# Scores and second GEMM on half-height row tiles of TensorE, with the steps, the sums and the last transposed x put in a new order

## The chip, the cores and the metric

One core of one Trainium2 chip. The metric is the device time of the whole kernel in microseconds, the median of several executions. Besides the times I use one profiled execution of each kernel. From its trace I take one number above all, which I call the **pitch** of a block: from the start of its first score matmul to the start of the next block's. It lets a change in one block be read apart from the other blocks. (Block 7 has no next block; its attention half takes as long as those of blocks 3 to 6.)

## The reference, cut to what matters

Decayed causal attention over 8 batches of 8 heads (576 tokens, head size 64), then a feed-forward layer of 512 to 2048 to 512 with exact GELU over all 4608 tokens.

```python
scores = scale * np.matmul(q, k.transpose(0, 1, 3, 2))      # q, k: (8, 8, 576, 64)
decay = cum[:, :, :, None] - cum[:, :, None, :]             # cum = cumsum(log f)
scores = np.where(causal, -1000000000.0, scores + decay)
attn = softmax(scores)                                      # over the keys
x = np.matmul(attn, v)  ->  (4608, 512)
h = x @ w_in                                                # 512 -> 2048
out = (0.5 * h * (1.0 + erf(h * inv_sqrt2))) @ w_out        # 2048 -> 512
```

## The kernel before

The program walks over blocks: block b is batch b. Each block has an attention half and a half in which TensorE runs the first GEMM of that block and ScalarE the GELU. The second GEMM of block b-1 is cut into 64 single matmuls of 512 columns, and these *steps* are dealt out among the score tiles of block b, so that TensorE has work while ScalarE takes the exponentials. Two heads lie in one 128-partition tile, one in each half. A score has a contraction of 64, so the other half of the query tile is zeroed and each head gets a full 128-row matmul:

```python
qA = [consts.tile([P, S], BF16, name=f"qA{i}") for i in range(HP)]   # lower half zero
qB = [consts.tile([P, S], BF16, name=f"qB{i}") for i in range(HP)]   # upper half zero
kT = [consts.tile([P, S], BF16, name=f"kT{i}") for i in range(HP)]

def scores(b, i, t):                       # head pair i, tile t of 4
    st = s_psum.tile([P, 2, 512], FP32, tag="s", name=f"s{t}")       # two buffers
    c = 0
    for n, q0, w in STILES[t]:             # 256+192, 320+128, 448, 320 columns
        for h, qt in enumerate((qA[i], qB[i])):
            nc.tensor.matmul(st[:, h, c : c + w], kT[i][:, K0[n] : K0[n] + P],
                             qt[:, q0 : q0 + w], ...)
        ...                                # block 0 and pair 0 of block 1: mask matmuls, 128 rows
        c += w
    nc.scalar.activation(et[:, :, 0:c], st[:, :, 0:c], Act.Exp, scale=scale)
    ...                                    # else: the mask by GpSimd on et
```

```python
def gemm2(c, quarters=False):              # a generator: one step at each yield
    ...
        nc.tensor.matmul(pss[ts], g_of[c][kt][:, ts * P : (ts + 1) * P],
                         w_out_sb[:, kt, :], start=(kt == 0), stop=(kt == n_ff - 1))
        if kt == n_ff - 1:
            nc.vector.tensor_copy(ot, pss[ts]);  nc.sync.dma_start(out[...], ot)
        yield

FILL = [[4, 6, 2, 2], [2, 2, 2, 2], [2, 2, 2, 2], [2, 2, 1, 1], [8, 0, 20]]
# steps after tile t of pair i; the attention product of pair i-1 goes in three pieces
# after tiles 1, 2 and 3 of pair i; the last x goes through a transposing DMA under 20 steps
```

Block 1 has its own table of steps, as its weights still arrive. The last piece, the tails of 64 tokens, follows after block 7 and isn't touched.

The softmax here doesn't subtract the row's maximum and nothing guards it: scores larger than these inputs give would overflow.

## Time and profile before

| | before |
|---|---|
| time, median of 3 | 357.31 us (356.77 to 357.79) |
| TensorE busy | 97% of the span |
| pitch of blocks 1, 2, 3 to 7 | 40.81, 38.14, 37.42 us |
| attention half and first GEMM of a block from 3 on | 23.53 and 13.89 us |
| VectorE and ScalarE busy in such an attention half | 9.37 and 16.23 us |

How to read it: matmuls are pipelined, so the lengths in a timeline overlap (a 512-column matmul lasts 379 ns and the next starts after 216). I read prices from starts. A share of 97% says only that TensorE always has something in flight. The prediction shows the lines.

### The profile page before, as it was taken

To read this page: it belongs to the slowest core of one execution; us is meant where nothing else is said; L and a number is where in the kernel's file an instruction comes from. 1 tells how busy PE (TensorE), PEld (TensorE's weight loads), DVE (VectorE), ACT (ScalarE), POOL (GpSimd) and SP (SyncE) were. 2 spreads that over 40 slices of the span, in tenths; PEclk is the share of its full clock that TensorE was granted. 3 is DMA by queue.
4 is the path that set the end of the run, shared out by engine and by line. 5 is a ranking of instruction groups with operands and counts; after the bars stand their busy time and mean duration, and the time that the engine had idled before them with its cause. 6 is when DMAs were issued, how large, how long until landed. Compare 5 with 4: busy or idle time off the path is not lost.

```text
span 356.2 us, 7069 instructions
## 1 busy us (share of the span) xinstructions
PE 346.8 (97%) x2756; PEld 190.7 (54%) x2756; DVE 182.1 (51%) x482; ACT 217.4 (61%) x298; POOL 124.5 (35%) x243
## 2 busy tenths in 40 slices
PE   8998989999999999999999999999999999999995
PEld 3784556544664466445654565446544664444443
DVE  6771984595467625781559145924584361011011
ACT  5697586368854797279826882688457854603600
POOL 7390275406546044804470256215520530000000
PEclk9999999999999999999999999999999999999999
DMA  7999999885997894489639973979310132011013
GB/s 116 169 188 191 190 155 202 183 192 90 205 158 161 146 185 122 95 142 189 144 98 134 188 139 82 174 141 173 76 66 2 45 61 81 2 59 59 2 30 88
DMA packets 103936, 43.85 MB, mean 123 GB/s; under 512 B 82720, under 2 KB 99360, under 8 KB 103904
## 3 DMA queue, kind: packets, MB, share of 16 engines
q1 hardware_dynamic: 86608, 29.26, 40.4%
q0 software_dynamic: 16896, 13.63, 25.6%
q10 hardware_dynamic: 400, 0.52, 0.4%
q8 instruction: 21, 0.34, 0.4%
q14 instruction: 11, 0.09, 0.1%
HBM read 36.85 MB, written 9.44 MB: 130 GB/s over the span
## 4 chain that ended last, share of the span: by engine, by line
PE 94%; ACT 2%; DMA 1%; issue 1%; DVE 1%; POOL 0%; ACTq 0%; DVEq 0%; POOLq 0%
PE ps L404 35%; PE ps L442 35%; PE s L308 13%; PE o L344 8%; ACT e L323 2%; PE ps_f L198 1%; DMA k<-in_k_dram 1%; PE s L317 1%; PE ps_w L187 1%; PE ps_x L380 0%; PE s_t L233 0%; PE ps_t L233 0%; DVE x L360 0%; ACT xt L368 0%; ACT g L416 0%
## 5 line engine op out<-in xcount | busy, mean ns | idle before, releaser
L416 ACT ACTIVATE g<-ps 128x512 bf16<-128x512 f32 x144 | 86.0, 597 | 97.9 <-PE ps L404 97.8
L442 PE MATMUL ps<-w_out_sb,g 128*128 128x512 bf16 (+2 forms) x592 | 143.8, 373 | 0.0
L323 ACT ACTIVATE e<-s 128x896 bf16<-128x896 f32 (+1 forms) x128 | 105.1, 863 | 19.8 <-PE s L308 11.3
L404 PE MATMUL ps<-xT,w_in_sb 128*128 128x512 bf16 x512 | 112.9, 379 | 0.7 <-ACT xT L383 0.6
L325 POOL TENSOR_SCALAR_AFFINE_SELECT e<-e 128x256 bf16<-128x256 bf16 x135 | 53.7, 408 | 118.6 <-ACT e L323 117.7
L404 PEld LDWEIGHTS <-w_in_sb 128*128 128x128 bf16 x576 | 56.0, 97 | 69.2 <-issue 3.9
L451 DVE COPY ot<-ps 128x512 f32<-128x512 f32 (+2 forms) x37 | 25.1, 677 | 105.3 <-PE ps L442 105.0
L442 PEld LDWEIGHTS <-g 128*128 128x128 bf16 x592 | 52.2, 98 | 41.8
L292 POOL TENSOR_TENSOR vw<-v_sb,wT 128x640 bf16<-128x640 f32 x32 | 41.0, 1282 | 45.7 <-PE ps_t L233 15.9
L308 PEld LDWEIGHTS <-kT 128*128 128x128 bf16 x384 | 36.7, 98 | 33.3 <-issue 6.2
L308 PE MATMUL s<-qA,kT 128*128 128x256 bf16 (+2 forms) x192 | 51.9, 282 | 2.1 <-ACT e L323 2.0
L308 PE MATMUL s<-qB,kT 128*128 128x256 bf16 (+2 forms) x192 | 48.6, 282 | 0.0
L344 PE MATMUL o<-vw,e 128*128 128x65 bf16 x960 | 43.5, 194 | 0.5 <-ACT e L323 0.4
L344 PEld LDWEIGHTS <-e 128*128 128x128 bf16 x960 | 39.5, 98 | 7.5 <-ACT e L323 0.5
L359 DVE RECIPROCAL r<-o 128x5 f32<-128x5 f32 x64 | 12.5, 195 | 41.5 <-PE o L344 41.0
L276 DVE COPY kT<-tk 64x288 bf16<-64x288 bf16 x96 | 32.3, 336 | 1.4
L360 DVE TENSOR_TENSOR x<-o,r 128x256 bf16<-128x256 f32 x64 | 27.2, 425 | 2.4 <-DVE r L359 0.2
L276 DVE COPY qB<-tq 64x288 bf16<-64x288 bf16 x48 | 18.8, 391 | 0.6
L370 DVE TENSOR_SCALAR xt<-o,r 64x64 bf16<-64x64 f32 x60 | 17.5, 291 | 1.4
L276 DVE COPY qA<-tq 64x288 bf16<-64x288 bf16 x48 | 17.1, 355 | 1.1
L404 PE MATMUL ps<-tails,w_in_sb 128*128 128x512 bf16 x64 | 14.4, 377 | 0.0
L416 ACT ACT_TABLE_LOAD x8 | 10.3, 1283 | 0.1
(63 smaller groups left out, 124.4 us busy)
## 6 DMA issues: line engine op xcount, KB each, us to landing
out_dram<-ot SPq DMA_DIRECT2D x32, 256.0 KB, 2.2
v_sb<-in_v_dram SPq DMA_DIRECT2D x20, 256.0 KB, 4.7
v_sb<-in_v_dram SPq DMA_DIRECT2D x29, 128.0 KB, 5.4
q<-in_q_dram POOLq DMA_DIRECT2D x6, 576.0 KB, 6.6
k<-in_k_dram POOLq DMA_DIRECT2D x6, 576.0 KB, 9.0
w_in_sb<-in_moe_w_in_dram POOLq DMA_DIRECT2D x4, 512.0 KB, 7.6
w_out_sb<-in_moe_w_out_dram POOLq DMA_DIRECT2D x4, 512.0 KB, 9.6
q<-in_q_dram POOLq DMA_DIRECT2D x4, 144.0 KB, 4.1
```

The lines of the kernel that those rows point to most:

```text
L276: nc.vector.tensor_copy(rows[:, odd], src[odd * D : (odd + 1) * D, 2 * i + h].rearrange("d j p -> d p j"),)
L292: nc.gpsimd.tensor_tensor(vw_of[b][:, hs, :, 0:D], v_sb[:, hs, :, :], w.unsqueeze(3).to_broadcast([P, 2, NBLK, D]), Alu.mult,)
L308: nc.tensor.matmul(st[:, h, c : c + w], kT[i][:, K0[n] : K0[n] + P], qt[:, q0 : q0 + w], start=True, stop=not on_pe or c not in SDIAG[t],)
L323: nc.scalar.activation(et[:, :, 0:c], st[:, :, 0:c], Act.Exp, scale=scale)
L325: nc.gpsimd.affine_select(out=et[:, :, c0 : c0 + P], in_=et[:, :, c0 : c0 + P], compare_op=Alu.is_ge, fill=0.0, base=0, pattern=[[0, 2], [ ...
L344: nc.tensor.matmul(o[:, m, :], e_of[b, i, t][:, h, c : c + P], vw_of[b][:, 2 * i + h, n, :], start=(n == 0), stop=(n == m),)
L360: nc.vector.tensor_tensor(x_of[b, i][:, :, h, :], o[:, 0:4, 0:D], r[:, 0:4].unsqueeze(2).to_broadcast([P, NBLK - 1, D]), Alu.mult,)
L370: nc.vector.tensor_scalar(*tail, r[D:P, 4:5], None, Alu.mult)
L404: nc.tensor.matmul(ps, w_in_sb[:, kt, ffb * P : (ffb + 1) * P], src[:, kt, :], start=(kt == 0), stop=(kt == n_dm - 1),)
L416: nc.scalar.activation(g_of[c][ffb], ps, Act.Gelu)
L442: nc.tensor.matmul(pss[ts][:, c0:c1], g_of[c][kt][:, ts * P : (ts + 1) * P], w_out_sb[:, kt, c0:c1], start=(kt == 0), stop=(kt == n_ff - 1),)
L451: nc.vector.tensor_copy(ot[:, c0:c1], pss[ts][:, c0:c1])
```

## The change

The intent: a head's score needs only 64 of the array's 128 rows, so two heads can use the upper and the lower half at the same time. But a change between whole-height and half-height matmuls costs time (0.095 us in the trace before; I call it a drain), so the steps dealt out between score tiles are made half-height as well: each contraction of 128 is split into two of 64 ("r"), summed in two banks (parts of the memory that TensorE writes to), and VectorE adds the two for each token tile (128 tokens of the output). A few steps ("n") stay whole, where they stand beside the attention product, which is whole.

```diff
-    qA = [consts.tile([P, S], BF16, name=f"qA{i}") for i in range(HP)]
-    qB = [consts.tile([P, S], BF16, name=f"qB{i}") for i in range(HP)]
+    qT = [consts.tile([P, S], BF16, name=f"qT{i}") for i in range(HP)]
...                                        (zeroing memsets go; copies of q write qT)
-            for h, qt in enumerate((qA[i], qB[i])):
+            for h in range(2):
+                d = slice(h * D, (h + 1) * D)
                 nc.tensor.matmul(
                     st[:, h, c : c + w],
-                    kT[i][:, K0[n] : K0[n] + P],
-                    qt[:, q0 : q0 + w],
+                    kT[i][d, K0[n] : K0[n] + P],
+                    qT[i][d, q0 : q0 + w],
...
+    STEPS = [
+        16 * "r",
+        5 * "r" + 2 * "n" + 8 * "r" + "n",
+        9 * "r" + 2 * "n" + 5 * "r",
+        8 * "r" + 8 * "n",
+    ]
+    def gemm2_rows(c):
+        for ts, steps in enumerate(STEPS):
+            ...                            (two banks: of o for ts 0, of m for 1 and 2, of s for 3)
+            for kt, step in enumerate(steps):
+                last = kt == steps.rindex("r")
+                for r in range(2 if step == "r" else 1):
+                    rows = slice(r * D, (r + 1) * D) if step == "r" else slice(0, P)
+                    nc.tensor.matmul(banks[r], g_of[c][kt][rows, ...], w_out_sb[rows, kt, :], ...)
+                if kt == n_ff - 1 if ts == n_sub - 1 else last:
+                    nc.vector.tensor_copy(ot, banks[1])
+                if kt == n_ff - 1:
+                    nc.vector.tensor_tensor(ot, ot, banks[0], Alu.add)
+                    nc.sync.dma_start(out[...], ot)
+                yield
...
-    FILL = [[4, 6, 2, 2], [2, 2, 2, 2], [2, 2, 2, 2], [2, 2, 1, 1], [8, 0, 20]]
+    FILL = [[6, 5, 4, 3], [0, 3, 3, 2], [0, 3, 3, 3], [0, 3, 3, 2], [8]]
+    FILL_AV = [2, 1, 2, 2]
...
+        def av(i):                         (whole product of a pair, after tile 1 of the next)
+            for h in range(2):
+                attend(b, i, h, (0, 1, 2, 3, 4))
+                if h == 0:
+                    take(fill, FILL_AV[i])
+                normalize(b, i, h)
...
-            x_dma(b, i)                    (last x, blocks 3 to 7; 20 steps behind it)
+        av(HP - 1)
+        take(fill, 5)
+        to_xT(b, HP - 1, nc.vector.tensor_copy, o_psum, "o")     (four transposes, one copy)
+        take(fill, 999)                                          (one step)
```

Blocks 0 and 1 get the half-height scores too, but block 1 keeps its old order and, as its steps, the whole-height second GEMM of block 0. The second GEMM of block 7, behind all attention, stays whole-height too.

More of the change, by code (lines that the diff above doesn't have):

```diff
@@ L142 @@
     make_identity(nc, ident_fp)
-    qA = [consts.tile([P, S], BF16, name=f"qA{i}") for i in range(HP)]
-    qB = [consts.tile([P, S], BF16, name=f"qB{i}") for i in range(HP)]
+    qT = [consts.tile([P, S], BF16, name=f"qT{i}") for i in range(HP)]
     kT = [consts.tile([P, S], BF16, name=f"kT{i}") for i in range(HP)]
-    def zero_halves(pairs):
-        for i in pairs:
-            nc.vector.memset(qA[i][D:P, :], 0.0)
-            nc.vector.memset(qB[i][0:D, :], 0.0)
     w_in_sb = consts.tile([P, n_dm, d_ff], BF16)
@@ L174 @@
     nc.vector.memset(ones, 1.0)
-    zero_halves(range(2))
     nc.vector.memset(wT[0:D, 4, :], 0.0)
@@ L202, in transposes_first @@
                 )
-        def evac(eng, dst, r0, r1):
-            op = eng.copy if eng is nc.scalar else eng.tensor_copy
-            op(
-                dst[r0:r1, :].rearrange("d (p j) -> d p j", j=JT),
-                ps[r0:r1].rearrange("d j p -> d p j"),
-            )
-        if which:
-            evac(nc.vector, kT[i], 0, P)
-        else:
-            evac(nc.vector if i else nc.scalar, qA[i], 0, D)
-            evac(nc.vector, qB[i], D, P)
+        op = nc.scalar.copy if i == 0 and not which else nc.vector.tensor_copy
+        op(
+            (qT, kT)[which][i].rearrange("d (p j) -> d p j", j=JT),
+            ps.rearrange("d j p -> d p j"),
+        )
     def transposes_pe(b, i, pool):
@@ L239, in transposes_pe @@
             for h in range(2):
-                dst = (qA[i], qB[i])[h] if which == 0 else kT[i]
+                dst = (qT, kT)[which][i]
                 rows = dst[h * D : (h + 1) * D, :].rearrange(
@@ L270, in untangle @@
             for h in range(2):
-                dst = (qA[i], qB[i])[h] if which == 0 else kT[i]
+                dst = (qT, kT)[which][i]
                 rows = dst[h * D : (h + 1) * D, :].rearrange(
@@ L461, in gemm2 @@
             yield
+    STEPS = [
[6 more added lines that the diff above has]
+        for ts, steps in enumerate(STEPS):
+            if ts < n_sub - 1:
+                pool, tag = (m_psum, "m") if ts else (o_psum, "o")
+                banks = [
+                    pool.tile([P, d_model], FP32, tag=tag, name="ps2")
+                    for _ in range(2)
+                ]
+            else:
+                both = s_psum.tile([P, 2, d_model], FP32, tag="s", name="ps2")
+                banks = [both[:, 0], both[:, 1]]
+            ot = o_pool.tile([P, d_model], FP32, tag="ot", name="ot")
+            for kt, step in enumerate(steps):
+                last = kt == steps.rindex("r")
+                for r in range(2 if step == "r" else 1):
+                    rows = slice(r * D, (r + 1) * D) if step == "r" else slice(0, P)
+                    nc.tensor.matmul(
+                        banks[r],
+                        g_of[c][kt][rows, ts * P : (ts + 1) * P],
+                        w_out_sb[rows, kt, :],
+                        start=(kt == 0),
+                        stop=last if r else kt == n_ff - 1,
+                    )
+                if kt == n_ff - 1 if ts == n_sub - 1 else last:
+                    nc.vector.tensor_copy(ot, banks[1])
+                if kt == n_ff - 1:
+                    nc.vector.tensor_tensor(ot, ot, banks[0], Alu.add)
+                    nc.sync.dma_start(
+                        out[c * S + ts * P : c * S + (ts + 1) * P, :], ot
+                    )
+                yield
     def take(gen, n):
@@ L481, in first_attention @@
         transposes(0, o_psum, "o")
-        zero_halves(range(2, HP))
         warm_up(4)
@@ L534, in first_attention, with attention, av, second_attention @@
         to_xT(0, 3, nc.vector.tensor_copy)
-    FILL = [[4, 6, 2, 2], [2, 2, 2, 2], [2, 2, 2, 2], [2, 2, 1, 1], [8, 0, 20]]
+    FILL = [[6, 5, 4, 3], [0, 3, 3, 2], [0, 3, 3, 3], [0, 3, 3, 2], [8]]
+    FILL_AV = [2, 1, 2, 2]
     FILL_1 = [[0, 4, 4, 0], [0, 2, 3, 3], [4, 4, 4, 4], [3, 3, 3, 3], [8, 0, 99]]
-    def attention(b, fill, counts):
+    def attention(b):
+        fill = gemm2_rows(b - 1)
+        def av(i):
+            for h in range(2):
[3 more added lines that the diff above has]
+                normalize(b, i, h)
+        for i in range(HP):
+            for t in range(4):
+                scores(b, i, t)
+                take(fill, FILL[i][t])
+                if i and t == 1:
+                    av(i - 1)
+                    if i < HP - 1 or b > 2:
+                        x_dma(b, i - 1)
+                if t == 1 and i == 0:
+                    load_v(b + 1)
+                if b > 2 and t == 0 and i < 2:
+                    transpose_dma(b + 1, 4 * i, 4 * i + 4)
+                if b == 2 and t == 1 and i == 1:
+                    transpose_dma(3, 0, 4)
+                    transpose_dma(3, 4, 8)
+        take(fill, FILL[HP][0])
+        if b == 2:
+            to_xT(b, HP - 2, nc.vector.tensor_copy, o_psum, "o")
+        av(HP - 1)
+        take(fill, 5)
+        to_xT(b, HP - 1, nc.vector.tensor_copy, o_psum, "o")
+        x_tail_dma(b)
+        take(fill, 999)
+    def second_attention():
+        b, fill, counts = 1, gemm2(0, True), FILL_1
         for i in range(HP):
@@ L552, in attention @@
                     normalize(b, i - 1, 1)
-                    if i < HP - 1 or b > 2:
+                    if i < HP - 1:
                         x_dma(b, i - 1)
-                if t == 1 and i == 0 and b > 1:
-                    load_v(b + 1)
-                if b > 2 and t == 0 and i < 2:
-                    transpose_dma(b + 1, 4 * i, 4 * i + 4)
-                if b == 2 and t == 3 and i == 1:
-                    transpose_dma(3, 0, 4)
-                    transpose_dma(3, 4, 8)
-                if b == 1 and (i, t) == (0, 2):
+                if (i, t) == (0, 2):
                     transposes_pe(1, 3, o_psum)
-                if b == 1 and i == 1 and t in (0, 2):
+                if i == 1 and t in (0, 2):
                     weigh_v(1, 2 + t // 2)
-                if b == 1 and t == 3:
+                if t == 3:
                     if i == 1:
@@ L573, in attention @@
         take(fill, counts[HP][0])
-        if b <= 2:
-            to_xT(b, i - 1, nc.vector.tensor_copy, o_psum, "o")
+        to_xT(b, i - 1, nc.vector.tensor_copy, o_psum, "o")
         attend(b, i, 0, (0, 1, 2, 3, 4))
@@ L580, in attention @@
         normalize(b, i, 1)
-        if b <= 2:
-            take(fill, 7)
-            to_xT(b, i, nc.vector.tensor_copy, o_psum, "o")
-        else:
-            x_dma(b, i)
+        take(fill, 7)
+        to_xT(b, i, nc.vector.tensor_copy, o_psum, "o")
         x_tail_dma(b)
-        if b == 1:
-            transpose_dma(2, 4, 8)
-            load_v(2, 4, 8)
+        transpose_dma(2, 4, 8)
+        load_v(2, 4, 8)
         take(fill, 999)
@@ L594 @@
             first_attention()
+        elif b == 1:
+            second_attention()
         else:
-            attention(b, gemm2(b - 1, b == 1), FILL_1 if b == 1 else FILL)
+            attention(b)
         if b == 0:
```

## The prediction

> **What bounds the kernel now.** I read the page first: the busy shares, then the chain of work that ended last. TensorE is busy for nearly the whole span and is 94% of the chain, in two GEMMs of equal weight, then the scores (L308) and the attention product (L344).
>
> ```profile
> PE 346.8 (97%) x2756; PEld 190.7 (54%) x2756; DVE 182.1 (51%) x482; ACT 217.4 (61%) x298; POOL 124.5 (35%) x243
> ...
> PE 94%; ACT 2%; DMA 1%; issue 1%; DVE 1%; POOL 0%; ACTq 0%; DVEq 0%; POOLq 0%
> PE ps L404 35%; PE ps L442 35%; PE s L308 13%; PE o L344 8%; ACT e L323 2%; PE ps_f L198 1%; DMA k<-in_k_dram 1%; PE s L317 1%; PE ps_w L187 1%; PE ps_x L380 0%; PE s_t L233 0%; PE ps_t L233 0%; DVE x L360 0%; ACT xt L368 0%; ACT g L416 0%
> ```
>
> A busy TensorE can still be a waiting one, so next come busy times by stretch (us; PE, weight loads, DVE, ACT, POOL), for the attention half of block 4 (with the second GEMM of block 3 among it) and for the first GEMM after it.
>
> ```profile
> 160.60:184.30 23.70, 23.70 (x234) 14.37 (x233) 9.37 (x27) 16.23 (x19) 12.11 (x26) 1.00 0.78 137
> 184.30:198.10 13.80, 13.80 (x66) 6.16 (x64) 11.86 (x33) 8.96 (x15) 3.11 (x5) 1.00 0.81 146
> ```
>
> TensorE has no hole, at full clock; ACT is busy 16.23 of 23.70 us and VectorE 9.37. So only TensorE work taken away counts there, until ACT's exponentials hold the scores back. The timeline of TensorE (start, length, group) gives the real price of each piece, because starts are true while lengths overlap:
>
> ```profile
> 160.65 0.27 PE L308 MATMUL s<-qA,kT 128*128 128x256 bf16 x1
> 160.76 0.27 PE L308 MATMUL s<-qB,kT 128*128 128x256 bf16 x1
> 160.87 0.25 PE L308 MATMUL s<-qA,kT 128*128 128x192 bf16 x1
> 160.95 0.25 PE L308 MATMUL s<-qB,kT 128*128 128x192 bf16 x1
> 161.03 1.03 PE L442 MATMUL ps<-w_out_sb,g 128*128 128x512 bf16 x4
> ...
> 162.28 1.46 PE L442 MATMUL ps<-w_out_sb,g 128*128 128x512 bf16 x6
> 163.73 0.35 PE L308 MATMUL s<-qA,kT 128*128 128x448 bf16 x1
> 163.91 0.35 PE L308 MATMUL s<-qB,kT 128*128 128x448 bf16 x1
> 164.10 0.59 PE L442 MATMUL ps<-w_out_sb,g 128*128 128x512 bf16 x2
> ```
>
> Score tile 0 takes 161.03-160.65 = 0.38 us, with the two heads strictly one after the other (0.11 us apart for 256 columns); tile 2 takes 164.10-163.73 = 0.37. Four 512-column matmuls elsewhere give the pitch of the second GEMM: x20 from 179.86 to 184.18, 0.216 us each. Six from 162.28 would end at 163.57; the next score starts at 163.73, so 0.16 us is a wait, for the first exponential. ACT's own timeline says why:
>
> ```profile
> 161.46 1.28 ACT L323 ACT_TABLE_LOAD   x1
> 162.76 6.74 ACT L323 ACTIVATE e<-s 128x896 bf16<-128x896 f32 x8
> ```
>
> Its table comes in at 162.76 and the tile-0 exponential lasts 0.92. Eight in a row take 6.74 us: some 0.81 us from one 896-column exponential to the next, about 0.7 for the 640-column one.
>
> The block repeats exactly: scores of blocks 3 to 7 start 37.42 us apart (123.23, 160.65, 198.07, ...): 23.53 of attention half and 13.89 of first GEMM. Block 2 takes 38.14 and block 1 40.81.
>
> **What the Trainium skill says.** "TensorE: Matmul & The Clock Gate", Part 3: Packing small matmuls — row/col tiling: matmuls in different row groups run at the same time, starting about 4 ns apart. No row pair runs in this trace, but column halves do: the 24 transposes of 96 columns from 13.15 take until 13.90, 0.75 us, where 24 in a row at the observed 43 ns (the same half's starts) would be 1.03. "TensorEngine Tiling (Array Packing)", Key Properties: changing the tiling mode drains TensorE. The trace has that and prices it:
>
> ```profile
> 11.40 0.28 PE L317 MATMUL s<-after,ident_bf 128*128 128x128 bf16 x2
> 11.61 0.52 PE L489 MATMUL psw<-ident_fp,f_sb 64*128 64x64 f32 x5
> 12.06 0.36 PE L308 MATMUL s<-qA,kT 128*128 128x448 bf16 x1
> ```
>
> The second 128-column mask matmul starts at 11.456; in one mode the next would follow 0.056 later, at 11.51. The first of a 64*128 mode comes at 11.61: 0.095 us lost. I find 0.095 at each of five such places (11.01, 11.61, 12.06, 13.15, 13.90), into the small mode and out of it. "PSUM — Partial Sum Buffer", PSUM bank collisions raise a hardware error: different row tiles may not write one bank at a time; so each half of a second-GEMM step needs its own bank. The same page, Specifications (TRN2): a VectorE instruction takes at most one tensor input from PSUM; so the two halves cost a copy and an add. The copy alone is 0.69 us now (L451, 692 ns).
>
> **The change, part by part**, for a block from 3 on.
> 1. Scores on row tiles. A head pair's four tiles take 0.38+0.38+0.37+0.27 = 1.41 us now; the two heads side by side take half. Four pairs: 4 x 0.705 = 2.82 us off TensorE.
> 2. The second GEMM. Of its 64 steps 51 are now "r", two 64-row matmuls side by side, 13 are "n". If a pair runs like one, the pitch stays 0.216: no gain and no loss. The late start of the second of a pair (4 ns by the skill) may or may not add to the pitch; 75 pairs with the scores are 0.30 us at worst. I book half, 0.15. This part saves nothing by itself: it is there so that scores and their filling share a mode.
> 3. Mode switches. Into rows at tile 0 of pair 0, out and in around each of the attention products 0, 1, 2, out before the last: 8 x 0.095 = 0.76 us.
> 4. The last x by TensorE in place of a DMA: four 128-column transposes, 4 x 0.055 = 0.22 us (blocks 3 to 7; block 2 has them already). The five steps ahead of them are 1.08 us, against reciprocal plus multiply (0.23+0.43) and two handovers of about 0.1: just hidden. The copy (0.43) lies behind the last step and three matmuls of the first GEMM, 0.86.
> 5. The add: 4 x 0.69 = 2.8 us more VectorE, 0.43 more for x. 9.37+3.2 of some 22.5 us: beside TensorE, except where a bank is waited for.
> 6. Waits for exponentials. The order is now: tile 2, three steps, tile 3, two or three steps, tiles 0 and 1 of the next pair back to back. Count from the start of tile 2, one exponential after another: its scores end at 0.35, the exponential runs 0.45 to 1.37; tile 3's follows at 1.26 and ends at 1.97. TensorE meanwhile does 0.19+0.65+0.14+0.43+0.19 = 1.60 and wants tile 1, whose buffer is free at 2.02: 0.4 us of wait. With three steps after tile 3 it is 0.2; at the first pair, with four and three, some 0.2. At the block's start the table load again holds tile 2: filling of eleven steps (2.38) plus 0.1+0.19+0.19 = 2.86 against an exponential over 3.08 after the scores' start: 0.2.
> 7. Banks of the third token tile (m): the add of the second tile starts about 0.48 after its last step's start and lasts 0.69 with its release, 1.2; TensorE is back after 0.22+0.48+0.10+0.19 = 1.0: 0.2 us.
> Waits: 0.4+0.2+0.2+0.2+0.2 = 1.2, less the 0.16 there now: 1.0.
> Net per block: -2.82+0.15+0.76+0.22+1.0 = -0.69 us; block 2 without the 0.22: -0.91. Six blocks: -4.4 us.
>
> Blocks 0 and 1 keep the 128-row second GEMM, and block 0 has 128-row mask matmuls between the scores. Scores save 8 x 0.705 = 5.6. Switches: ten per masked pair (five pairs), 22 for pairs 1 to 3 of block 1: 72 x 0.095 = 6.8. Some of both is absorbed, as TensorE waits there for exponentials (at 47.40 for 0.99, 50.66 for 0.47 us). The zeroing memsets (8 x 0.30) and one of three copies per pair (0.75) leave VectorE, but the first scores start at 8.67, when the four warm-up matmuls end too. I book +0.4.
>
> Sum: 357.3-4.4+0.4 = 353.3 us.
>
> **Rivals.**
> (a) Pairs don't run side by side, or only in part. Then 51 second-GEMM steps and all scores grow: serial pairs would add 51 x 0.216 = 11 us per block, some 65 us in all. Against it: the column halves above do overlap. If the overlap lost only 10%, it would be 51 x 0.02+0.3 = 1.3 us per block, and the time 359 to 361.
> (b) The waits of steps 6 and 7 are smaller than my count, because the order was tuned on the chip. Without them a block gains 1.7 us, ten in all: 347. For it: such a detailed order is seldom written without a measurement. Against it: the exponentials' 0.81 and 0.7 us are measured, and two score buffers are all there are.
> (c) The drain costs more where it lies between long matmuls and both halves must reload: at 0.2 us a block loses 0.84 more, a wash or a loss with blocks 0 and 1, 357 to 362. Against it: 0.095 at all five places, after 64, 96 and 128 columns alike.
> (d) VectorE's queue becomes the bound, with normalization behind the sums: a block would show waits of L344 for o. For it: copy and add (1.4 us) precede a normalization; against it: it has 10 us free.
>
> **Range and chances.** Step 1 is sure to 0.1 us per block if pairs overlap; switches to 0.3; waits to 0.6. That is some 0.65 a block, shared by six blocks of one form, so 4 us in all. 348.6 to 356.8 should hold 8 in 10. Over 2% faster means below 350.2, rival (b) in good part: 0.24. Slower than 364.5 needs rival (a): 0.04. Within 2%: 0.72.
>
> **What would show it.** The score groups as 64*128, the two heads' starts some 4 ns apart, score tile 0 taking 0.19 instead of 0.38; pair pitch 0.216 to 0.22; a gap of 0.095 at each switch; TensorE waits for exponentials of about 1 us per block before tile 1; block pitch 36.7 instead of 37.42; VectorE 12.5 us per attention half. If the block pitch falls by over 1.2 the waits were overcounted; if it rises, pairs cost more than one matmul or a drain more than 0.095.

## The result, and the profile after

| | before | after |
|---|---|---|
| time, median of 4 | 357.04 us (356.52 to 357.79) | 352.79 us (352.21 to 353.81) |
| pitch of block 1 | 40.81 | 41.34 |
| pitch of block 2 | 38.14 | 36.88 |
| pitch of blocks 3 to 7 | 37.42 | 36.57 |
| attention half, first GEMM (block 4) | 23.53, 13.89 | 22.66, 13.91 |

The ratio is 0.9882 (0.985 to 0.9915). Ratios here and below are the mean time of one kernel's fast runs over the mean of the other's fast runs of the same rounds, so they are not quite the ratio of the medians. Executions over 1.5% slower than the fastest of the same kernel are left out of the means. In later rounds on one chip (run e9) the changed kernel had 352.53 us and the kernel before 357.74: 0.9863. So the change is a little over 1% faster.

The page of the changed kernel, busy shares and chain:

```profile
PE 338.7 (97%) x3082; PEld 174.8 (50%) x3082; DVE 203.0 (58%) x499; ACT 216.1 (62%) x298; POOL 124.5 (36%) x243
...
PE 83%; ACT 9%; POOL 2%; issue 2%; DMA 2%; SPq 1%; DVE 0%; ACTq 0%; POOLq 0%
```

TensorE's share is the same 97%, so that number tells nothing. The chain does: ScalarE's part of it went from 2% to 9%, because exponentials now hold TensorE up. Busy times by stretch for the same two halves as in the prediction (us of stretch; PE, weight loads, DVE, ACT, POOL; clock, DMA share, GB/s):

```profile
158.20:180.90 22.70, 22.40 (x288) 12.87 (x288) 12.57 (x35) 16.06 (x19) 9.13 (x21) 1.00 0.88 159
180.90:194.80 13.90, 13.90 (x65) 6.16 (x63) 13.40 (x32) 8.96 (x15) 6.11 (x10) 1.00 0.67 108
```

VectorE has 12.57 us in place of 9.37, beside TensorE; the attention half is shorter by 0.9. The timeline of TensorE from the start of block 4 (start, length, group):

```profile
158.25 0.37 PE L296 MATMUL s<-qT,kT 64*128 64x256 bf16 x4
158.45 1.46 PE L479 MATMUL ps<-w_out_sb,g 64*128 64x512 bf16 x12
159.75 0.35 PE L296 MATMUL s<-qT,kT 64*128 64x320 bf16 x4
159.94 1.24 PE L479 MATMUL ps<-w_out_sb,g 64*128 64x512 bf16 x10
161.23 0.37 PE L296 MATMUL s<-qT,kT 64*128 64x448 bf16 x2
...
163.07 0.75 PE L296 MATMUL s<-qT,kT 64*128 64x256 bf16 x8
163.64 0.83 PE L479 MATMUL ps<-w_out_sb,g 64*128 64x512 bf16 x6
164.40 0.65 PE L332 MATMUL o<-vw,e 128*128 128x65 bf16 x15
...
165.32 0.64 PE L332 MATMUL o<-vw,e 128*128 128x65 bf16 x15
165.89 0.36 PE L296 MATMUL s<-qT,kT 64*128 64x448 bf16 x2
```

Five things can be read here. Tile 0 takes 158.45-158.25 = 0.20 us, where it took 0.38. Twelve half-height matmuls take 159.75-158.45 = 1.30 us, 0.216 for each two: a pair costs just what one whole matmul cost. Ten from 159.94 would end at 161.02; the next score starts at 161.23, a wait of 0.21 for the first exponential. Tiles 0 and 1 of pair 1 stand back to back and take 163.64-163.07 = 0.57, where their columns need 0.38: 0.19 of wait. And from half height to whole, 163.64 to 164.40, three pairs need 0.65 and took 0.76: a drain of about 0.1.

ScalarE's side, from its timeline of the same stretch:

```profile
158.97 1.28 ACT L311 ACT_TABLE_LOAD   x1
160.27 3.13 ACT L311 ACTIVATE e<-s 128x896 bf16<-128x896 f32 x4
163.56 1.73 ACT L311 ACTIVATE e<-s 128x896 bf16<-128x896 f32 x2 [0.16 <-PE s L296]
166.35 3.18 ACT L311 ACTIVATE e<-s 128x896 bf16<-128x896 f32 x4 [1.07 <-PE s L296]
```

It works in bursts: it idles 1.07 us while the attention product runs, and then four tiles come close together. TensorE waits for it in the burst and it waits for TensorE after. The sums show it as well, in the list of waits of the whole kernel (total us, times, longest), first before, then after:

```profile
PE s L308 <- ACT e L323: 2.0, 3, 1.0
```

```profile
PE s L296 <- ACT e L311: 3.4, 9, 1.0
```

The list leaves out the short ones; from starts in block 4 I count 0.21, 0.19 and 0.40 us for exponentials, and in pair 3 a fourth wait, 0.35 us on one half of the array and 0.18 on the other, which came later (step 7 at the end says why).

### The profile page after: what moved, and what is told of

It reads as the page before. It is cut to its first block, busy times and chain, and to the rows that moved or that the text cites. A ratio compares the mean times of both kernels' runs of the same rounds, so it can differ in the third digit from the quotient of the medians.

```text
span 350.2 us, 7729 instructions
## 1 busy us (share of the span) xinstructions
PE 338.7 (97%) x3082; PEld 174.8 (50%) x3082; DVE 203.0 (58%) x499; ACT 216.1 (62%) x298; POOL 124.5 (36%) x243
## 4 chain that ended last, share of the span: by engine, by line
PE 83%; ACT 9%; POOL 2%; issue 2%; DMA 2%; SPq 1%; DVE 0%; ACTq 0%; POOLq 0%
PE ps L392 36%; PE ps L479 18%; PE ps L430 12%; PE o L332 9%; PE s L296 7%; ACT e L311 5%; ACT L311 2%; DMA v_sb<-in_v_dram 2%; ACT g L404 1%; POOL vw L279 1%; PE ps_x L368 1%; SPq L114 1%; POOL k L102 1%; POOL q L102 0%; PE s L305 0%
## 5 line engine op out<-in xcount | busy, mean ns | idle before, releaser
L479 PE MATMUL ps<-w_out_sb,g 64*128 64x512 bf16 (+1 forms) x690 | 102.4, 376 | 0.0
L296 PE MATMUL s<-qT,kT 64*128 64x320 bf16 (+4 forms) x384 | 47.9, 282 | 4.0 <-ACT e L311 3.4
L479 PEld LDWEIGHTS <-g 64*128 64x128 bf16 (+1 forms) x690 | 37.7, 94 | 25.4 <-issue 1.6
L263 DVE COPY qT<-tq 64x288 bf16<-64x288 bf16 x96 | 45.1, 470 | 1.5
L430 PE MATMUL ps<-w_out_sb,g 128*128 128x512 bf16 (+2 forms) x208 | 44.3, 363 | 0.0
L487 DVE COPY ot<-ps 128x512 f32<-128x512 f32 x24 | 16.5, 689 | 36.0 <-PE ps L479 36.0
L439 DVE COPY ot<-ps 128x512 f32<-128x512 f32 (+2 forms) x13 | 8.4, 650 | 48.9 <-PE ps L430 48.7
L296 PEld LDWEIGHTS <-kT 64*128 64x128 bf16 x384 | 20.1, 94 | 28.7 <-issue 15.6
L347 DVE RECIPROCAL r<-o 128x5 f32<-128x5 f32 x64 | 12.5, 195 | 30.1 <-PE o L332 29.3
L430 PEld LDWEIGHTS <-g 128*128 128x128 bf16 x208 | 18.8, 98 | 18.9 <-issue 0.4
L489 DVE TENSOR_TENSOR ot<-ot,ps 128x512 f32<-128x512 f32 x24 | 16.5, 687 | 1.3
```

The lines of the kernel that those rows point to most:

```text
L263: nc.vector.tensor_copy(rows[:, odd], src[odd * D : (odd + 1) * D, 2 * i + h].rearrange("d j p -> d p j"),)
L296: nc.tensor.matmul(st[:, h, c : c + w], kT[i][d, K0[n] : K0[n] + P], qT[i][d, q0 : q0 + w], start=True, stop=not on_pe or c not in SDIAG[t],)
L430: nc.tensor.matmul(pss[ts][:, c0:c1], g_of[c][kt][:, ts * P : (ts + 1) * P], w_out_sb[:, kt, c0:c1], start=(kt == 0), stop=(kt == n_ff - 1),)
L479: nc.tensor.matmul(banks[r], g_of[c][kt][rows, ts * P : (ts + 1) * P], w_out_sb[rows, kt, :], start=(kt == 0), stop=last if r else kt == n ...
```

## The experiments

All kernels gave correct results. Pitches of all of them, in us, from one profiled execution each; times are medians of the executions in the fast state (in e1 and in e3 one of the four was slow):

| | block 1 | block 2 | blocks 3 to 7 | time, ratio to before |
|---|---|---|---|---|
| before | 40.81 | 38.14 | 37.42 | |
| changed | 41.34 | 36.88 | 36.57 | 352.79, 0.9882 |
| changed again (e9) | 41.60 | 37.01 | 36.57 | 352.53, 0.9863 |
| e1 scores alone | (slow) | (slow) | 37.64 | 359.43, 1.0032 |
| e2 all steps "r" | 41.34 | 38.70 | 38.47 | 363.02, 1.0128 |
| e3 steps moved | 41.61 | 38.83 | 35.76 | 349.13, 0.9718 |
| e4 order alone | 40.80 | 38.85 | 37.70 | 361.13, 1.006 |
| e5 last x by DMA | 41.96 | 38.28 | 37.86 | 359.0, 1.0054 |
| e6 block 1 whole | 40.90 | 38.06 | 36.57 | 352.62, 0.9865 |
| e7 sums behind | 41.34 | 37.58 | 37.36 | 357.03, 0.9984 |
| e8 all together | 40.89 | 36.80 | 35.57 | 348.05, 0.9741 |
| e10 with block 2's x | 40.89 | 36.54 | 35.57 | 346.38, 0.9688 |

The theory is that of the prediction: halved scores, less a drain of 0.095 us at each change between whole and half height, less waits for exponentials. The main rivals: the second GEMM needn't have been split, as drains are hidden (e1, e2); the new order and the last x gained the time (e4, e5); the waits are ScalarE's pace and can't be removed (e3).

### e1: half-height scores alone

```diff
-        fill = gemm2_rows(b - 1)
+        fill = gemm2(b - 1)
```

> Row-tiled scores and the new order as in the changed kernel, but the second GEMM of blocks 1 to 6 in 128-row matmuls on one bank, without sums on VectorE. Theory (a drain of 0.094 us at each change of mode, waits for exponentials the rest): 26 changes of mode per block in place of 8, so 18 x 0.094 = +1.7 us, of which some 0.7 us lie in the waits for exponentials that are there anyway; no wait for the second bank: +1.0 us per block, six blocks: about 358.5 us, slower than the changed kernel by 1.6% and no faster than the kernel before; block pitch 37.5. Rival (the drains are mostly hidden and the row-tiled second GEMM is not needed): 353 us or less, pitch 36.6 or less.

Measured: 359.35, 359.43 and 360.79 us. The profiled execution was a slow one (364.82, granted clock 0.991; in block 1 it was 0.93), so I use its blocks 3 to 7 only, where the clock was 1.00: pitch 37.64. The start of block 4 in its timeline:

```profile
166.32 0.36 PE L296 MATMUL s<-qT,kT 64*128 64x256 bf16 x4
166.62 1.47 PE L430 MATMUL ps<-w_out_sb,g 128*128 128x512 bf16 x6
```

Tile 0 now occupies 0.30 us to the next start, not 0.20: the drain stands there, and so at each tile with steps beside it. What follows: the split of the second GEMM, which gains nothing by itself, is what makes half-height scores pay. Without it they are no faster than the kernel before (ratio 0.9966 to 1.0098). Not all of the 1.07 us over the changed kernel's pitch is drains: 0.88 lie in the attention half, and 0.19 in the first GEMM (14.10 us in place of 13.91), whose fifth matmul waits for VectorE's copy of the last token tile. The half-height second GEMM closes that tile in other banks.

### e2: all steps half-height

```diff
-        5 * "r" + 2 * "n" + 8 * "r" + "n",
-        9 * "r" + 2 * "n" + 5 * "r",
-        8 * "r" + 8 * "n",
+        16 * "r",
+        16 * "r",
+        16 * "r",
```

> All 64 steps of the second GEMM of blocks 1 to 6 on row tiles, so the steps between the attention product's two heads, and around the last transposes, change the mode too: 20 changes per block in place of 8, the work the same. Theory: 12 x 0.094 = +1.13 us per block, +6.8 us in all: 359.6 us, pitch 37.7; if a step beside other drains hides some, 358. Rival (a drain counts only where weights can't be loaded ahead, and costs little between 65-column matmuls): under +2 us in all.

Measured: pitch 38.47, so +1.90 us where I had said +1.13. The changes of mode are as counted: 19 within the attention half, together 1.80 us lost, 0.095 each. Most of the rest is one wait that I hadn't seen coming: one half of the array starts its step 0.72 us after the other (175.13 and 174.41), where it was 0.17 in the changed kernel. Timeline of TensorE, block 4:

```profile
172.65 0.65 PE L332 MATMUL o<-vw,e 128*128 128x65 bf16 x15
173.23 0.39 PE L479 MATMUL ps<-w_out_sb,g 64*128 64x512 bf16 x2
173.56 0.64 PE L332 MATMUL o<-vw,e 128*128 128x65 bf16 x15
174.13 0.36 PE L296 MATMUL s<-qT,kT 64*128 64x448 bf16 x2
174.41 0.37 PE L479 MATMUL ps<-w_out_sb,g 64*128 64x512 bf16 x1
175.13 0.80 PE L479 MATMUL ps<-w_out_sb,g 64*128 64x512 bf16 x5 [0.35 <-DVE ot L489]
```

The step at 173.23 closes the second token tile. If it is an "r", copy and add both start after it, and the third tile's bank comes free only at 175.13. In the changed kernel this step is an "n": the second bank is closed one step earlier, and its copy runs under the first attention product. So the single "n" at the end of that row does two jobs: no change of mode, and a head start for the copy.

### e3: the same steps dealt out otherwise

```diff
-    FILL = [[6, 5, 4, 3], [0, 3, 3, 2], [0, 3, 3, 3], [0, 3, 3, 2], [8]]
+    FILL = [[6, 6, 4, 2], [1, 2, 3, 2], [2, 1, 3, 3], [1, 2, 3, 2], [8]]
```

> The changed kernel with the same steps dealt out otherwise: one or two of the steps after tile 1 stand between tiles 0 and 1, one more ahead of tile 2 at the block's start. Nothing else. Theory (TensorE waits about 1.0 us per block for exponentials because tiles 2, 3, 0, 1 come close together on two buffers): 0.7 to 0.9 us of it goes, pitch 35.8, 348.0 us. Rival (ScalarE's work as a whole sets these waits, so they reappear at the next tile): pitch 36.4 or more, 352 us.

Measured: pitch 35.76, as expected to 0.04 us; 349.13 us (the fourth execution, 354.02, was slow), ratio 0.9718 (0.9638 to 0.9799). TensorE between pairs 0 and 1:

```profile
164.63 0.36 PE L296 MATMUL s<-qT,kT 64*128 64x256 bf16 x4
164.82 0.39 PE L479 MATMUL ps<-w_out_sb,g 64*128 64x512 bf16 x2
165.22 0.37 PE L296 MATMUL s<-qT,kT 64*128 64x320 bf16 x4
165.41 0.61 PE L479 MATMUL ps<-w_out_sb,g 64*128 64x512 bf16 x4
```

One step between the tiles still leaves 165.22-164.82-0.216 = 0.18 us of wait; where two stand (pair 2) there is none. What follows: the waits were the order's, not ScalarE's pace. ScalarE is busy 16.00 us of the shorter half as before. The time gained less than five blocks at 0.81 and block 2 should give, since block 2 took 38.83 in the profiled execution. The entry for the transposed x in that stretch says why (what it waited for, in us and times):

```profile
  DMA xT<-x: 2.7, 1
```

TensorE's first GEMM of block 2 waited 2.7 us for a transposing DMA. Of the profiled executions with the new order, the changed kernel's two and those of e2, e7 and e10 had no such wait, or next to none (0.06 us in e9), and it was 0.8 to 1.3 in e1, e4, e5, e6 and e8. The kernel before had none in its profile either. I take it to come from the other loads of that stretch, but didn't isolate it.

### e4: the new order alone

The kernel before, with the changed kernel's `attention(b)` and `second_attention()` and the whole-height `gemm2(b - 1)` as its steps.

> The kernel before (128-row scores with zeroed halves, 128-row second GEMM on one bank) with the new order of attention and the last x by TensorE. Theory: no change of mode, no gain from pairs; +0.22 us transposes and +0.2 us more wait for exponentials per block, +2.3 us in all: 359.5 us, pitch 37.8. Rival (order and last x are what gained): 353 us.

Measured: 361.13 us, ratio 1.006 (0.9992 to 1.0128); pitch 37.70. The order and the last x by TensorE gain nothing by themselves. Of the 0.28 us of pitch, 0.16 lie in the attention half (23.69 us), which now holds the transposes' 0.22, and 0.12 in the first GEMM (14.01): its fifth matmul waits 0.20 us for VectorE's copy of the last token tile, where it waited 0.08 in the kernel before, because the copy of the transposed x now goes ahead on VectorE. (This trace lacks 46 matmul records; the starts used here are in it.)

### e5: the last x by DMA again

```diff
         av(HP - 1)
+        if b > 2:
+            x_dma(b, HP - 1)
         take(fill, 5)
-        to_xT(b, HP - 1, nc.vector.tensor_copy, o_psum, "o")
+        if b == 2:
+            to_xT(b, HP - 1, nc.vector.tensor_copy, o_psum, "o")
```

> The changed kernel, but the last x of blocks 3 to 7 goes through the transposing DMA as before, started right after the last normalization, with the six steps left behind it. Theory: the DMA lands some 2.5 us after its issue and the multiply it waits for ends 0.9 us after the last attention matmul; six steps and three matmuls of the first GEMM cover 1.95 us, the four transposes (0.22) go: a wait of 1.2 to 1.5 us before the fourth matmul of the first GEMM, pitch 37.8 in blocks 3 to 7, about 358.9 us. Rival (the transposes were a plain cost): pitch 36.35, 351.7 us.

Measured: 359.0 us (ratio 1.0054), pitch 37.81 to 37.92. TensorE at the end of block 4's attention half:

```profile
182.17 0.64 PE L332 MATMUL o<-vw,e 128*128 128x65 bf16 x15
182.65 1.46 PE L479 MATMUL ps<-w_out_sb,g 128*128 128x512 bf16 x6
183.94 0.81 PE L392 MATMUL ps<-xT,w_in_sb 128*128 128x512 bf16 x3
186.17 1.02 PE L392 MATMUL ps<-xT,w_in_sb 128*128 128x512 bf16 x4 [1.41 <-DMA xT<-x]
```

The fourth matmul of the first GEMM starts at 186.17, 1.58 us after its turn, which was three times 0.216 behind 183.94 (the 1.41 in the line counts from the end of the third). The DMA that it waits for was issued at 183.61. So with only six steps left behind the last product the DMA can't be hidden. Four transposes for 0.22 us are what allows the steps to be spent earlier, among the scores.

### e6: block 1 with whole-height scores

Zeroed halves `qA` and `qB` for block 1 alone, filled by its transposes, cleared in the first GEMM of block 0:

```diff
-                d = slice(h * D, (h + 1) * D)
+                d = slice(0, P) if b == 1 else slice(h * D, (h + 1) * D)
+                qt = (qA, qB)[h][i] if b == 1 else qT[i]
```

> The changed kernel, with the scores of block 1 alone in 128-row matmuls on zeroed halves as before (its second GEMM is in 128-row matmuls in both kernels, so there each tile changed the mode twice). Theory: block 1 goes back from 41.34 to 40.8 us; all else stays: 352.3 us, which the times alone can't tell from the changed kernel; the pitch of block 1 decides. Rival (block 1 is slower for another reason, such as its loads): 41.3.

Measured: block 1 takes 40.90 us, against 41.34 and 41.60; 352.62 us, not to be told from the changed kernel. So where the neighbours are whole-height, as in block 1, half-height scores lose. In the changed kernel's block 1 each tile is drained on both sides:

```profile
58.09 0.31 PE L296 MATMUL s<-qT,kT 64*128 64x320 bf16 x2
58.34 0.65 PE L332 MATMUL o<-vw,e 128*128 128x65 bf16 x15
58.82 1.03 PE L430 MATMUL ps<-w_out_sb,g 128*128 128x512 bf16 x4
59.78 0.37 PE L296 MATMUL s<-qT,kT 64*128 64x256 bf16 x4
```

The 320-column pair needs 0.14 and has 0.25 to the next start; the four steps need 0.86 and have 0.96.

### e7: the sum behind the normalization

```diff
                 attend(b, i, h, (0, 1, 2, 3, 4))
+                normalize(b, i, h)
                 if h == 0:
                     take(fill, FILL_AV[i])
-                normalize(b, i, h)
```

> The changed kernel, but on VectorE the normalization of a pair's first head goes ahead of the sum that closes a token tile, not behind it. Theory: the sum of the second token tile ends 0.4 to 0.9 us later, so the third tile's first bank comes free later; the 64-row half that needs it waits 0.6 to 1.0 us in place of 0.17, of which 0.25 lies in the wait for the exponential that follows: +0.5 us per block, pitch 37.1, 355.8 us. Rival (VectorE's order doesn't matter, it has 10 us free): pitch 36.6.

Measured: 357.03 us (ratio 0.9984), pitch 37.36, +0.79 where I had said +0.5. VectorE's closing add and then TensorE, block 4:

```profile
173.33 0.69 DVE L489 TENSOR_TENSOR ot<-ot,ps 128x512 f32<-128x512 f32 x1
```

```profile
173.11 0.38 PE L479 MATMUL ps<-w_out_sb,g 64*128 64x512 bf16 x1
174.07 0.80 PE L479 MATMUL ps<-w_out_sb,g 64*128 64x512 bf16 x5 [0.59 <-DVE ot L489]
```

One half starts its first step at 173.11 in its free bank; the other waits until 174.07, 0.96 us. The free half doesn't get far: its second step comes behind the waiting one in the program and starts only at 174.08, so both halves lose. A VectorE with 10 us free in a stretch of 23 still costs TensorE 0.8 us per block, by the order of two things in its queue. So the sum ahead of the normalization is worth as much as nearly all of the change's net gain.

### e8: all together

The steps in e3's manner with two between tiles 0 and 1 of every pair (`[[6, 6, 4, 2], [2, 1, 3, 2], [2, 1, 3, 3], [2, 1, 3, 2], [8]]`), the step that closes the second token tile ahead of the attention product, and block 1 as in e6.

> The steps moved as in e3, now two between tiles 0 and 1 of every pair; the step that closes the second token tile ahead of the attention product, so that its sum comes earlier; block 1 in 128-row scores as in e6. Theory: the waits left in e3 (0.19, 0.13 and 0.18 us) go: pitch 35.4, block 1 40.8: 346.5 us. Rival (what is left is ScalarE's pace): pitch 35.7, 348 us.

Measured: pitch 35.57, not 35.4; block 1 40.89; 348.05 us, with two runs at 346.2 and two at 350 (granted clock 0.995 there). All waits for exponentials are gone from block 4. The wait of 0.17 us for the third tile's bank stayed, so that part of the edit failed. VectorE's timeline shows the copy from 166.41 to 167.10 and the add at 167.20: the closing step (166.30) was early enough, but the add has to wait for the copy ahead of it, which couldn't start before the last half-height step was done.

### e9 and e10: the changed kernel again, and the second x of block 2

e10 is e8 with two edits for block 2 only: no transposing DMA for its second x, and four more transposes on TensorE.

> The changed kernel itself once more, on the same chip and in the same rounds as the next, to compare the two without the spread between chips: 352.5 to 353.5 us, pitch of blocks 3 to 7 at 36.57.

> As e8, and the second x of block 2 by TensorE too, since its DMA, behind the loads on one queue, made the first GEMM of block 2 wait 0.8 to 2.9 us in some profiles (e3, e6, e8) and not in others. Theory: block 2 takes 36.2 us in every execution in place of 36.8 to 38.8, blocks 3 to 7 stay at 35.57: 345.8 us, 2.0% under the changed kernel, and less spread. Rival (the wait moves to another load of that stretch): block 2 at 36.8 or more, 348 us.

Measured in the same rounds: 352.53 us for the changed kernel, 346.38 (346.13 to 347.44) for e10, ratios 0.9863 and 0.9688 to the kernel before. 346.38 is 1.7% under the changed kernel and 3.1% under the kernel before. Block 2 took 36.54, a third of a microsecond over what I expected, with no wait for a DMA in this execution; one execution can't show that it never has one. The four runs lie within 1.3 us, e8's within 4.2, but e8's spread went with a lower clock, so I don't credit it to this edit.

## Why the prediction was right, point by point

The predicted 353.3 us against 352.79 and 352.53: inside the range, and the mechanism holds step by step. Some sizes were off: the lag of a pair (step 2), the waits that were there before the change (below), and blocks 0 to 2.

1. **Halved scores.** Said: 2.82 us per block. Tile 0 takes 0.20 in place of 0.38, tile 1 0.19 in place of 0.38. Right.
2. **A pair costs one matmul.** Said: pitch 0.216, with perhaps 4 ns more per pair, booked as 0.15 us. Two half-height steps start 2 to 4 ns apart, or, once a wait for an exponential has parted the halves, 17 to 21 (23 of the 51 in block 4; six more lie further apart, after the wait of step 7); the pitch is 0.216 either way, so the lag isn't paid at each pair. It shows at a drain into whole height, which counts from the later half: some 20 ns at each of four, 0.08 us. Rival (a) is out.
3. **Eight drains of 0.095.** In block 4 each lost between 0.091 and 0.097 us, counted from the later half, in both directions, beside 65-, 448- and 512-column matmuls. e2 shows the same price on twice as many. Rival (c) is out.
4. **The last x.** Said: 0.22 us and just hidden. Right; e5 shows what it avoids.
5. **VectorE's adds beside TensorE.** 12.57 us busy against 12.5 said. But rival (d) had a point that I underrated: not the load of the queue counts, but its order (e7: 0.79 us per block).
6. **Waits for exponentials.** Said: 0.2, 0.2, 0.4, 0.2. Measured: 0.21, 0.19, 0.40, and for the one before pair 3's tile 1 0.35 on the leading half, 0.18 on the other. That they are the order's own was not in the prediction, and rival (b) had it the wrong way round: I asked whether a tuned order would have avoided them; e3 shows that it could have, and hadn't.
7. **The third token tile's bank.** Said: 0.2 us of TensorE. Measured: 0.17 us of one half of the array. The other half went on, as its own next step was due only 0.216 us later, and came 0.17 us earlier to the next wait, for an exponential, which released both. So along either half the two waits come to 0.35 us, where 0.4 was said, and the bank by itself cost nothing in the changed kernel. All waits together: 1.16 us along either half, 1.2 said.

Net per block: said -0.69, measured -0.85 us (attention half -0.87, first GEMM +0.02). The 0.15 of step 2 was too much. And the prediction booked only one wait of the kernel before, 0.16 us, where its trace has two more that go away: 0.11 ahead of tile 0 of pair 1 (two steps from 164.81 end at 165.24, the score starts at 165.34), and 0.08 in the first GEMM, whose fifth matmul stood until VectorE had copied the last token tile. With the 0.15 these come to 0.34 us, and the shorter waits after the change to 0.04. Some 0.2 go the other way: the 0.08 of lag in step 2, and gaps of a few ns each that I don't place.

The prediction takes two rules on PSUM, the memory of the banks, from the Trainium skill (a bank for each half, one input from there for a VectorE instruction). Every kernel here keeps to them, so no run tests them.

**Blocks 0 and 1**, said +0.4. Block 1 alone: +0.53, and e6 takes it back. Block 0 can't be read from the two profiles: its first GEMM starts at 28.75 before and 27.83 after, but also at 27.47 in e4, whose block 0 is the old one, and at 29.1 in e7 and e10, whose block 0 is the new one. The difference is in the four warm-up matmuls ahead of the first scores, which take 1.89 us in some executions and 1.04 in others. Counted from the first transposes to the first GEMM, among quick starts the old code took 21.87 (e4) and the new one 21.80 to 22.41; among slow ones the old 23.04 and the new 23.44 and 23.52. So block 0 gained nothing by the change, or lost up to half a microsecond.

**Block 2**: said -0.91, measured -1.26 and, in e9, -1.13. Most of the surplus over the other blocks is a wait that only the kernel before had: ahead of the last attention product of block 2 TensorE stood for 0.28 us, until 104.33, while VectorE copied the transposed x (103.85 to 104.27) out of a bank.

That the sum came within 0.8 us is in part luck: blocks 2 to 7 gained about 1.1 us more than was said, block 1 and perhaps block 0 lost up to 0.6 more, and the warm-up alone moves an execution by 0.85.

What stays open: the waits for the transposing DMA in block 2, which come and go between executions.

## What to carry to other kernels

When two contractions of 64 can share the array, the gain is half of their columns, and each change of tiling mode takes 0.095 us off it: so first see whether the neighbours can be brought into the same mode, even where that gains them nothing. Then read the waits again, because a faster producer meets the same consumers: here a few steps dealt out otherwise (e3) gained nearly as much per block (0.81 us) as the whole change (0.85). And an engine with half its time free can still hold up the bound one by the order of its queue.

## What the Trainium skill lacked or had wrong

- "TensorEngine Tiling (Array Packing)", Key Properties, says that a change of tiling mode drains TensorE, without a price. Here it is 0.091 to 0.097 us per change, between 128*128 and 64*128 in either direction (and 96*64 in the first block), after matmuls of 64 to 512 columns.
- "TensorE: Matmul & The Clock Gate", Part 3: Packing small matmuls — row/col tiling, says that matmuls are strictly in program order in start and end, without reordering. Between two row tiles this trace shows otherwise for the starts (ends are modelled in it). In the changed kernel both L296 matmuls below come before the L479 ones behind them in the program; yet one half of the array began its next step at 171.11, before the other half began its score at 171.15, because that half had waited 0.17 us for a bank (timeline of TensorE, block 4). A matmul that waits still held back those behind it: in e7 the free half's second step started 6 ns after the step that had waited 0.96 us. The lines of the changed kernel:

```profile
170.98 0.29 PE L296 MATMUL s<-qT,kT 64*128 64x320 bf16 x1
171.11 0.38 PE L479 MATMUL ps<-w_out_sb,g 64*128 64x512 bf16 x1
171.15 0.29 PE L296 MATMUL s<-qT,kT 64*128 64x320 bf16 x1
```

- The same part gives 3.07 times for four row tiles of 32 rows, and no measured figure for two of 64. For these, back to back with 512 columns, the runs show twice the rate in full (0.216 us per pair against 0.216 per whole matmul), with both halves' weight loads (94 ns each) hidden.
- The pages say that row tiles need different banks, but none has a price for joining the two sums: here 0.69 us for the copy plus 0.69 for the add of a 128x512 tile on VectorE, in series.
